# Two blocks of gate and value as plain fp32 products, with the conversions moved behind two root chains

## The chip, the cores and the metric

The kernel runs on one core of a Trainium2 chip. The metric is the device time of one execution in microseconds (us). The engines are TensorE (PE: matmuls; PEld: its weight loads), VectorE (DVE), ScalarE (ACT), GpSimd (POOL) and SyncE (SP, which issues the DMAs).

## The reference

Attention over pooled keys and values, then a gated feed-forward layer behind a root-mean-square norm, then a second feed-forward layer with two factors:

```python
k_p, v_p = mean of 8 neighbouring keys / values         # 576 -> 72 per head
attn = softmax(q @ k_p.T / 8) @ v_p                     # 4 batches, 8 heads, head size 64
x = attn as (2304 tokens, 512)
xn = x / sqrt(mean(x * x) + 1e-6) * rms_g
g = xn @ w_gate;  y = (silu(g) * (xn @ w_val)) @ w_out  # 512 -> 1536 -> 512
out = ((y @ w_a) * (y @ w_b)) @ w_out2                  # 512 -> 1536 -> 512
```

The weights arrive as 64-bit floats. The chip reads each as two 32-bit words and puts an fp32 number together from them.

## The kernel before

The first layer runs over five tiles of 512, 256, 512, 512 and 512 tokens, and in each over 12 blocks f of 128 hidden columns. The attention works in units of 256 tokens; the first tile is made of units 0 and 1, and its left half (`ha`) can be multiplied as soon as unit 0 is scaled.

**Weights.** Block f has three parts (gate, value, out). A part is loaded by SP into one of four staging tiles `st`, and `load_part` can use a tile again only when the conversion four parts earlier has ended. The conversion (`c` in the order list) is two ACT instructions (lines 590 and 591), two on DVE (597 and 600) and one on POOL (607). For the products as three terms, a part is then split (`split_w`, lines 621 and 622) into a high half on ACT and a low half on POOL, or on DVE where the order list writes `!`. The splits have two buffers for gate and two for value.

**Product.** `half` (line 804) multiplies a split weight with split tokens: low by high, high by high, high by low, three matmuls in the reduced type for each 128 rows. Where `f < DIRECT` it multiplies the plain weight with the plain tokens, one fp32 matmul. DIRECT is 0. The first tile's out projection (`out_direct`, line 675) is fp32 already, of the same 128x256 shape in the first four jobs. The jobs 0 to 3 of the first tile are block 0 left, block 1 left, block 0 right, block 1 right; job 4 is block 2 over all 512 tokens, and so on. In the order list g, a, v, h, o stand for the gate product, its silu, the value product, their multiplication on DVE (line 818, into tile `ht`) and the out projection of a job.

**The root chain.** `narrow_rsqrt` (steps V0.6 and V1.6) finds one over the root of the mean square of 256 tokens: three small DVE instructions (478, 481, 485), nine more in three Newton steps (491 to 493), two that make a diagonal (464). V0.7 and V1.7 let PE spread the diagonal (line 472) and then scale the tokens on DVE (line 529). The squares of unit 1 in odd chunks lie in the same buffer `nr` as the diagonal of unit 0. `x0` and `x1` split the scaled tokens of the two units (lines 636 and 637).

**Order.** FIRST lists the steps of the first tile. A step without a sign is free, and its last instruction on each engine becomes the mark; a step with `-` or `=` has its ACT, DVE and POOL instructions put behind the mark of their engine. A planner then orders each engine's queue within these edges, and the engines run their queues in order. `p0` to `p6` pool the second batch's keys and values, the even ones on DVE (line 189), those with `!` on POOL.

Of the kernel before, what the change touches and what calls it, by code (L numbers as in the profile page):

```python
# [20 lines left out]
SLICE = 768  # L21
HALF = SLICE // 2
FINE = 2
DIRECT = 0

# [4 lines left out]
FIRST = """  # L32
=k0 -A0.0@att =k1 l -k2! k3 -l t0@att =A0.1@acc1 A0.2@att w0 =A0.5@acc0 =A0.6@acc3 =A0.7@acc3
-w1 A0.3 =A0.4 w2 t1 =A0.8 A1.0@att A1.1@acc0 A0.9! =c l =A1.2@v -V0.0@acc0 A1.5@acc2 -A1.3
-V0.1@acc1 c A1.6@acc3 s0.0 -V0.2@acc0,v A1.4! -V0.3@g,acc0 =A1.7@acc1 A1.8 A1.9 V0.4@acc2,att
=V0.5@att -c =V1.0@acc0 =V0.6 =V0.7@v =V1.1@g -x0! -g0a V1.2@att,acc3 =V1.3@acc2,acc1 c =g0b
-V1.4@acc0,att =l V1.5@acc2 =V1.6 =V1.7@acc0 s0.1! =c =x1 -a0 s1.0 =v0a =v0b -c =h0 =o0 -g1a
-g1b -s1.1! =c L0 -a1 A2.0 -g2a v1a =L1 -g2b p0 =p1! v1b =c s2.0! h1 =c =a2 =c g3a =c v2a =v2b
-h2 =c g3b =o1 a3 =p2 =o2 -v3a =v3b -s2.1 -h3 g4a g4b p3! -c a4 -v4a s3.0 =c -p4 -v4b s3.1! =c
=o3 =g5a =p5! =c =h4 c -c s4.0! -g5b -c -a5 s4.1! v5a -s5.0 v5b -h5 -g6a -o4 -g6b a6 -p6 -c  # L40
=v6a p7 -s5.1 =v6b -A2.1 -g7a -c =g7b -h6 =c =M0 -c =A2.2 =c -A2.3 =s6.1! =s6.0! -a7 o5 -c v7a
=c =A2.4 v7b s7.0! -h7 -g8a -g8b =a8 -o6 s7.1! c =v8a A2.5 c =s8.0 =p8 v8b =g9a -V2.0 g9b -h8
-a9 -o7 v9a =g10a -s9.0 v9b -c =s8.1 -h9 =c =V2.1 =o8 -V2.2 g10b =s9.1! -a10 -c V2.3 =v10a
-V2.4 -c v10b s10.0 g11a -g11b -h10 =a11 =V2.5 =c -s10.1 =c =o9 -g12a =c -v11a s11.0 =A3.0
=g12b -v11b h11 =a12 -V2.6 -v12a -g13a c -o10 A3.1 -v12b -o11 =g13b -s11.1 =A3.2 -A3.3 =M1
-h12 a13 -v13a -V2.7 -v13b =o12 -h13 =A3.4 =o13 =A3.5
""".split()
SECOND = """
A4.0 =r0 -r1 r2 -r3 r4 -r5 V3.0 r7 =r6 =r8 -V3.1 =V3.2 N0 =V3.3 A4.1 -N1
# [14 lines left out]
def attention_moe_moe2(  # L64
# [715 lines left out]
    def first_tile():  # L780
# [8 lines left out]
        def half(j, part, c0):  # L789
            f, cols, last = jobs[j]  # L790
            if f < DIRECT:
                terms = ((wf[0, f, part], xf_t[0]),)
# [529 lines left out]
```

## Time and profile before

| what | value |
|---|---|
| median of three runs | 1028.63 us (1025.25 to 1029.28) |
| profiled execution, its own time | 1028.68 us |
| its span, first to last instruction | 1026.9 us |
| PE busy | 984.9 us, 96% |
| DVE busy | 608.1 us, 59% |
| ACT busy | 437.9 us, 43% |
| POOL busy | 369.5 us, 36% |
| POOL line 622 (low halves of weights) | 121 instructions, 1366 ns each |

Busy shares are means over the whole run. The stretch that the change touches is about 35 to 90 us, and there the engines stand differently to each other than over the run, so it is read by stretches.

### The profile page before, as it was taken

Reading aid. Unit: us, or ns where it says so; the run is one execution under the profiler, and the core shown is the slowest. Engines: PE = TensorE matmul, PEld = TensorE weight load, DVE = VectorE, ACT = ScalarE, POOL = GpSimd, SP = SyncE. Lnnn points to the kernel's source line nnn. Section 1 sums busy time; section 2 is a strip of 40 time slices with the busy share of each in tenths; the row PEclk is TensorE's granted clock in tenths of the full one; section 3 lists DMA queues with packets and bytes.
Section 4 is the critical chain, followed back from the end, with each engine's and each line's share of the span. In section 5 each row is a group of like instructions: output and inputs, shape, how many; then the busy total and the mean of one; then the engine's idle time right before and its main releaser. Section 6 shows DMA issues by size and latency. Waiting matters only on the chain. (4 is left out here: it accounts for less than half of the span.)

```text
span 1026.9 us, 13276 instructions
## 1 busy us (share of the span) xinstructions
PE 984.9 (96%) x4820; PEld 845.0 (82%) x4820; DVE 608.1 (59%) x963; ACT 437.9 (43%) x822; POOL 369.5 (36%) x301
## 2 busy tenths in 40 slices
PE   4988999999999989999999999999999999999998
PEld 3776676778888877888788899999999998888886
DVE  6898966564733765363627759766776665322221
ACT  3845661232534545444445445434444434331211
POOL 6476672100153433443348620533344333310000
PEclk9889999999999999999999999999999999999999
DMA  8556543320100002000112133444443444643431
GB/s 227 156 175 194 178 140 105 102 78 1 41 1 21 1 1 62 1 1 1 41 28 75 42 111 113 139 148 135 140 151 125 130 129 178 203 140 118 139 113 72
DMA packets 82801, 101.53 MB, mean 99 GB/s; under 512 B 24112, under 2 KB 63024, under 8 KB 82736
## 3 DMA queue, kind: packets, MB, share of 16 engines
q1 hardware_dynamic: 82736, 100.69, 31.7%
q8 instruction: 38, 0.62, 0.2%
q14 instruction: 27, 0.22, 0.1%
HBM read 73.93 MB, written 26.74 MB: 98 GB/s over the span
## 5 line engine op out<-in xcount | busy, mean ns | idle before, releaser
L622 POOL TENSOR_TENSOR wl<-wf,wh 128x512 fp32r<-128x512 f32 x121 | 164.4, 1366 | 263.0 <-ACT wh L621 255.3
L621 ACT CAST wh<-wf 128x512 fp32r<-128x512 f32 x132 | 80.2, 619 | 76.2 <-PE acc L667 27.4
L1103 DVE TENSOR_TENSOR hl<-hf,hh 128x768 fp32r<-128x768 f32 x36 | 35.5, 992 | 95.1 <-ACT hh L1102 95.1
L1125 PE MATMUL o<-woh,hl 128*128 128x512 f32 x216 | 85.8, 397 | 0.0
L1125 PE MATMUL o<-woh,hh 128*128 128x512 f32 x216 | 85.0, 394 | 0.0
L1125 PE MATMUL o<-wol,hh 128*128 128x512 f32 x216 | 84.7, 392 | 0.0
L607 POOL TENSOR_TENSOR w<-w,st 128x512 int32<-128x512 int32 x24 | 31.9, 1330 | 116.0 <-DVE w L600 114.8
L1102 ACT CAST hh<-hf 128x768 fp32r<-128x768 f32 x36 | 29.8, 834 | 91.4 <-PE o L1125 81.5
L675 PE MATMUL acc<-ht,wf 128*128 128x256 f32 (+1 forms) x208 | 67.0, 465 | 1.2 <-DVE ht L818 0.7
L607 POOL TENSOR_TENSOR wf<-wf,st 128x512 int32<-128x512 int32 x36 | 52.9, 1475 | 39.0 <-DVE wf L600 17.3
L1240 ACT ACTIVATE ht<-g 128x512 f32<-128x512 f32 (+1 forms) x48 | 26.1, 544 | 92.8 <-PE g L654 90.2
L1248 DVE TENSOR_TENSOR ht<-ht,v 128x512 f32<-128x512 f32 (+1 forms) x48 | 29.6, 617 | 56.2 <-PE v L654 54.9
L667 PE MATMUL acc<-hh,wl 128*128 128x512 f32 x144 | 57.7, 400 | 3.5 <-ACT hh L1257 3.5
L654 PE MATMUL v<-xh,wl 128*128 128x512 f32 x144 | 57.9, 402 | 0.0
L667 PE MATMUL acc<-hl,wh 128*128 128x512 f32 x144 | 56.8, 394 | 0.1
L654 PE MATMUL g<-xh,wl 128*128 128x512 f32 x144 | 56.7, 394 | 0.0
L667 PE MATMUL acc<-hh,wh 128*128 128x512 f32 x144 | 56.6, 393 | 0.0
L654 PE MATMUL v<-xl,wh 128*128 128x512 f32 x144 | 56.3, 391 | 0.0
L654 PE MATMUL g<-xh,wh 128*128 128x512 f32 x144 | 56.2, 390 | 0.0
L654 PE MATMUL v<-xh,wh 128*128 128x512 f32 x144 | 56.1, 390 | 0.0
L654 PE MATMUL g<-xl,wh 128*128 128x512 f32 x144 | 56.1, 390 | 0.0
L1032 ACT COPY p<-X 128x384 f32<-128x384 f32 x36 | 17.3, 480 | 90.1 <-PE X L1024 90.1
(212 smaller groups left out, 2731.5 us busy)
## 6 DMA issues: line engine op xcount, KB each, us to landing
hf<-h SPq DMA_DIRECT2D x36, 384.0 KB
st<-in_moe_w_out_dram SPq DMA_DIRECT2D x24, 512.0 KB
h<-u SPq DMA_DIRECT2D x36, 192.0 KB
h<-p SPq DMA_DIRECT2D x36, 192.0 KB
st<-in_moe_w_gate_dram SPq DMA_DIRECT2D x12, 512.0 KB
st<-in_moe_w_val_dram SPq DMA_DIRECT2D x12, 512.0 KB
st<-in_moe_w_a_dram SPq DMA_DIRECT2D x12, 512.0 KB
st<-in_moe_w_b_dram SPq DMA_DIRECT2D x12, 512.0 KB
```

The source lines that it names most:

```text
L607: nc.gpsimd.tensor_tensor(out=bits, in0=bits, in1=low, op=ALU.add)
L621: nc.scalar.copy(wh, wf[ph, f, i])
L622: (nc.vector if boot["alt"] else nc.gpsimd).tensor_sub(wl, wf[ph, f, i], wh.bitcast(F32))
L654: nc.tensor.matmul(bank[:, :n], w[:, c, :], x[:, c, cols], start=(i == 0), stop=(i == len(terms) * KD - 1),)
L667: nc.tensor.matmul(accs[c][:, cols], w[:, c, :], x[:, :n], start=(f == 0 and i == 0 and cols.start == 0), stop=(f == NF - 1 and i == 2),)
L675: nc.tensor.matmul(accs[c][:, cols], wf[0, f, 2][:, c, :], ht[:, :cols.stop - cols.start], start=(f == 0 and cols.start == 0), stop=(f == ...
L1032: nc.scalar.copy(t, src[:, :HALF])
L1102: nc.scalar.copy(hh, hf)
L1103: nc.vector.tensor_sub(hl, hf, hh.bitcast(F32))
L1125: nc.tensor.matmul(accs[i], x[:, sub], y, start=(f == 0 and j == 0), stop=(f == NF - 1 and j == 2),)
L1240: act = nc.scalar.activation(out=ht[:, :m], in_=gb[:, :m], func=AF.Silu)
L1248: nc.vector.tensor_mul(ht[:, :m], ht[:, :m], vb[:, :m])
```

## The change

`DIRECT` goes from 0 to 2: jobs 0 to 3 multiply plain fp32 gate and value weights with the plain scaled tokens, one matmul in place of three. The splits of those four parts (s0.0, s0.1, s1.0, s1.1) leave the order list. `x0` and `x1` move from before jobs 0 and 1 to behind job 1's value product, since block 2 is now the first to use split tokens. The steps V0.6, V0.7, V1.6 and V1.7 lose their `=`: they are no longer held behind the mark, and they become it. So all that follows with a sign, the conversions among it, stands behind them, and `p0` gets a sign (`-p0`) and stands behind them too.

```diff
-DIRECT = 0
+DIRECT = 2
...
--V0.1@acc1 c A1.6@acc3 s0.0 -V0.2@acc0,v A1.4! -V0.3@g,acc0 =A1.7@acc1 A1.8 A1.9 V0.4@acc2,att
-=V0.5@att -c =V1.0@acc0 =V0.6 =V0.7@v =V1.1@g -x0! -g0a V1.2@att,acc3 =V1.3@acc2,acc1 c =g0b
--V1.4@acc0,att =l V1.5@acc2 =V1.6 =V1.7@acc0 s0.1! =c =x1 -a0 s1.0 =v0a =v0b -c =h0 =o0 -g1a
--g1b -s1.1! =c L0 -a1 A2.0 -g2a v1a =L1 -g2b p0 =p1! v1b =c s2.0! h1 =c =a2 =c g3a =c v2a =v2b
--h2 =c g3b =o1 a3 =p2 =o2 -v3a =v3b -s2.1 -h3 g4a g4b p3! -c a4 -v4a s3.0 =c -p4 -v4b s3.1! =c
+-V0.1@acc1 c A1.6@acc3 -V0.2@acc0,v A1.4! -V0.3@g,acc0 =A1.7@acc1 A1.8 A1.9 V0.4@acc2,att
+=V0.5@att -c =V1.0@acc0 V0.6 V0.7@v =V1.1@g -g0a V1.2@att,acc3 =V1.3@acc2,acc1 c =g0b
+-V1.4@acc0,att =l V1.5@acc2 V1.6 V1.7@acc0 =c -a0 =v0a =v0b -c =h0 =o0 -g1a -g1b =c L0 -a1
+A2.0 -g2a v1a =L1 -g2b -p0 =p1! v1b =c s2.0! h1 =c =a2 =c -x0! g3a =c v2a =v2b =x1 -h2 =c g3b
+=o1 a3 =p2 =o2 -v3a =v3b -s2.1 -h3 g4a g4b p3! -c a4 -v4a s3.0 =c -p4 -v4b s3.1! =c =o3 =g5a
```

The rest of the list is the same steps in the same order.

## Rows read from the trace of the kernel before

**Rows 1.** Stretches of time: length, each engine's busy us, granted clock, DMA.

```profile
core 0: us, PE busy (x) PEld busy (x) DVE busy (x) ACT busy (x) POOL busy (x), PEclk, DMA share, GB/s
...
56.30:63.10 6.80, 6.28 (x28) 5.81 (x27) 5.27 (x5) 1.52 (x3) 5.55 (x6) 0.50 0.65 195
63.10:75.20 12.10, 12.10 (x75) 10.54 (x73) 11.32 (x17) 8.91 (x17) 7.16 (x6) 1.00 0.53 170
75.20:87.00 11.80, 7.61 (x33) 6.08 (x34) 11.70 (x12) 6.99 (x13) 10.35 (x9) 1.00 0.70 216
...
90.50:112.40 21.90, 21.89 (x94) 14.77 (x93) 17.32 (x26) 10.92 (x18) 13.13 (x10) 1.00 0.64 194
```

**Rows 2.** Waits of PE from 80 to 200 us: total, times, longest.

```profile
PE v L804 <- DVE ht L818: 2.8, 1, 2.8
```

**Rows 3.** Timeline of PE: start, us, instruction, idle before and its releaser.

```profile
54.96 0.70 PE L472 MATMUL rb<-dg,ones 128*128 128x256 f32 x2 [1.99 <-DVE dg L464]
...
67.40 3.62 PE L675 MATMUL acc<-ht,wf 128*128 128x256 f32 x16
...
71.21 0.28 PE L804 MATMUL v<-xh,wl 128*128 128x256 f32 x1
...
72.17 0.28 PE L804 MATMUL v<-xl,wh 128*128 128x256 f32 x1
...
76.62 0.47 PE L804 MATMUL v<-xh,wl 128*128 128x512 f32 x1 [1.42 <-DVE ht L818]
```

**Rows 4.** Timeline of DVE, 34 to 64 us.

```profile
34.86 0.16 DVE L478 TENSOR_SCALAR ba<-sq 128x4 f32<-128x4 f32 x1
...
39.91 0.48 DVE L464 TENSOR_SCALAR dg<-ident,br 128x128 f32<-128x128 f32 x2
...
43.80 0.16 DVE L478 TENSOR_SCALAR ba<-sq 128x4 f32<-128x4 f32 x1 [1.22 <-PE sq L434]
...
57.38 1.21 DVE L529 TENSOR_TENSOR xf<-xf,rb 128x1024 f32<-128x1024 f32 x1
59.28 3.01 DVE L637 TENSOR_TENSOR xl<-xf,xh 128x512 fp32r<-128x512 f32 x2 [0.69 <-ACT xh L636]
63.84 0.42 DVE L818 TENSOR_TENSOR ht<-ht,v 128x256 f32<-128x256 f32 x1 [1.56 <-PE v L804]
```

**Rows 5.** Timeline of DVE, 86 to 164 us.

```profile
86.14 0.68 DVE L818 TENSOR_TENSOR ht<-ht,v 128x512 f32<-128x512 f32 x1
...
98.85 0.43 DVE L597 TENSOR_SCALAR wf<-wf 128x512 int32<-128x512 int32 x1 [4.42 <-ACT wf L590]
...
159.63 0.15 DVE L478 TENSOR_SCALAR ba<-sq 128x4 f32<-128x4 f32 x1
...
163.20 0.48 DVE L464 TENSOR_SCALAR dg<-ident,br 128x128 f32<-128x128 f32 x2
```

**Rows 6.** Groups by form on DVE, 44 to 94 us: count, busy us, mean ns.

```profile
L600 DVE SCALAR_TENSOR_TENSOR wf<-st,wf 128x512 int32<-128x512 int32 x14 | 15.0, 1069 | 0.2
...
L622 DVE TENSOR_TENSOR wl<-wf,wh 128x512 fp32r<-128x512 f32 x5 | 3.4, 683 | 0.0
L491 DVE TENSOR_TENSOR by<-br 128x4 f32<-128x4 f32 x3 | 2.4, 790 | 0.0
...
L492 DVE TENSOR_TENSOR by<-by,ba 128x4 f32<-128x4 f32 x3 | 1.5, 495 | 0.0
```

**Rows 7.** Timeline of ACT: two waits for PE.

```profile
41.18 0.38 ACT L425 ACTIVATE sq<-xT 128x256 f32<-128x256 f32 x1 [1.11 <-PE rb L472]
...
63.54 0.62 ACT L621 CAST wh<-wf 128x512 fp32r<-128x512 f32 x1 [3.78 <-PE g L804]
```

**Rows 8.** Timeline of SP: the load of block 2's out weights.

```profile
43.51 0.34 SPq L572 DMA_DIRECT2D st<-in_moe_w_out_dram  x1
```

**Rows 9.** Timeline of POOL: a split of block 1, a conversion of block 2.

```profile
43.44 1.28 POOL L622 TENSOR_TENSOR wl<-wf,wh 128x512 fp32r<-128x512 f32 x1
...
66.98 1.37 POOL L607 TENSOR_TENSOR wf<-wf,st 128x512 int32<-128x512 int32 x1 [3.57 <-DVE wf L600]
```

More of the change, by code (lines that the diff above doesn't have):

```diff
@@ L34 @@
 -w1 A0.3 =A0.4 w2 t1 =A0.8 A1.0@att A1.1@acc0 A0.9! =c l =A1.2@v -V0.0@acc0 A1.5@acc2 -A1.3
--V0.1@acc1 c A1.6@acc3 s0.0 -V0.2@acc0,v A1.4! -V0.3@g,acc0 =A1.7@acc1 A1.8 A1.9 V0.4@acc2,att
-=V0.5@att -c =V1.0@acc0 =V0.6 =V0.7@v =V1.1@g -x0! -g0a V1.2@att,acc3 =V1.3@acc2,acc1 c =g0b
--V1.4@acc0,att =l V1.5@acc2 =V1.6 =V1.7@acc0 s0.1! =c =x1 -a0 s1.0 =v0a =v0b -c =h0 =o0 -g1a
--g1b -s1.1! =c L0 -a1 A2.0 -g2a v1a =L1 -g2b p0 =p1! v1b =c s2.0! h1 =c =a2 =c g3a =c v2a =v2b
--h2 =c g3b =o1 a3 =p2 =o2 -v3a =v3b -s2.1 -h3 g4a g4b p3! -c a4 -v4a s3.0 =c -p4 -v4b s3.1! =c
[L40 to L46, printed above, removed]
+-V0.1@acc1 c A1.6@acc3 -V0.2@acc0,v A1.4! -V0.3@g,acc0 =A1.7@acc1 A1.8 A1.9 V0.4@acc2,att
[3 more added lines that the diff above has]
+=o1 a3 =p2 =o2 -v3a =v3b -s2.1 -h3 g4a g4b p3! -c a4 -v4a s3.0 =c -p4 -v4b s3.1! =c =o3 =g5a
+=p5! =c =h4 c -c s4.0! -g5b -c -a5 s4.1! v5a -s5.0 v5b -h5 -g6a -o4 -g6b a6 -p6 -c =v6a p7
+-s5.1 =v6b -A2.1 -g7a -c =g7b -h6 =c =M0 -c =A2.2 =c -A2.3 =s6.1! =s6.0! -a7 o5 -c v7a =c
+=A2.4 v7b s7.0! -h7 -g8a -g8b =a8 -o6 s7.1! c =v8a A2.5 c =s8.0 =p8 v8b =g9a -V2.0 g9b -h8 -a9
+-o7 v9a =g10a -s9.0 v9b -c =s8.1 -h9 =c =V2.1 =o8 -V2.2 g10b =s9.1! -a10 -c V2.3 =v10a -V2.4
+-c v10b s10.0 g11a -g11b -h10 =a11 =V2.5 =c -s10.1 =c =o9 -g12a =c -v11a s11.0 =A3.0 =g12b
+-v11b h11 =a12 -V2.6 -v12a -g13a c -o10 A3.1 -v12b -o11 =g13b -s11.1 =A3.2 -A3.3 =M1 -h12 a13
+-v13a -V2.7 -v13b =o12 -h13 =A3.4 =o13 =A3.5
 """.split()
```

## The prediction

> **What bounds the kernel now.** The page says PE, 96% busy over the span, so anything that shortens PE's work or its pauses for good should shorten the run. That is a mean, though, and I first read the table of stretches. From 90.5 to 112.4 us PE is busy 21.89 of 21.90 us, and DVE 17.32. From 75.2 to 87.0 it is the other way round: DVE 11.70 of 11.80, PE only 7.61; from 63.1 to 75.2 both are nearly full [rows 1]. So up to about 87 us the run is bound by DVE, whose queue holds the weight conversions, and after that by PE. Second, PE's waits name the place where the two meet: the value product of block 3 waits 2.8 us for the hidden product `ht` of block 2 [rows 2], which DVE reaches at 86.14 [rows 5]. From 87 us on there is slack on DVE: at 98.85 it has sat idle 4.42 us for ACT [rows 5]. Nothing behind that is set by a clock time of its own, so what DVE gains by 86.14 us, PE keeps to the end, if PE itself can be early by as much.
>
> Third, the DVE timeline shows what is in its queue. The root chain of unit 1 begins at 43.80 and its scaled tokens are there at 58.59, 14.8 us later; in a later unit the same 14 instructions of the chain, with nothing between, take 159.63 to 163.68, 4.05 us [rows 4, 5]. In between stand conversions, pooling, splits. PE waits 1.99 us for the end of that chain [rows 3], and in 56.3 to 63.1 runs at a granted clock of 0.50, the lower level of 1.2 GHz [rows 1].
>
> **The change, part by part.** The sum is made against the profiled execution, 1028.68 us, which is 0.05 us above the median shown.
>
> *PE's work.* Jobs 0 to 3 hold 4 x 2 x 4 = 32 products of 128x256. Three reduced matmuls cost 3 x 0.12 us (nine starts from 71.21 to 72.17 are eight steps in 0.96 us) = 0.36; one fp32 matmul costs 0.216, as 16 of the out projection take 3.62, of which the last is 0.38, so fifteen steps in 3.24 [rows 3]. Saved: 32 x 0.144 = 4.6 us at the full clock.
>
> The Trainium skill, page "FP8 and Floating Point Precision", section "TensorE Precision Notes", says that true FP32 takes four passes through the array. By that one fp32 product would cost four reduced matmuls, 0.48 us, and the change would add 32 x 0.12 = 3.8 us; the sixteen rows at 0.216 each, under two, speak against it.
>
> *PE's pauses.* The 1.99 us before the spreading [rows 3] goes with the shorter chain. The 1.42 us at 76.62, a wait for DVE's `ht` [rows 3], may go. The slow stretch from 56.3 holds 28 matmuls in 6.28 us busy, 0.224 each, against 75 in 12.10, 0.161, in the next at the full clock [rows 1]: 28 x 0.063 = 1.8 us if the clock doesn't fall. In all PE could be early by 4.6 + 2.0 + 1.4 + 1.8 = 9.8 us.
>
> *DVE up to 86.14 us*, which I hold to decide, since it is the later of the two:
> - Two of the four splits are DVE's (s0.1, s1.1): 2 x 0.68 [rows 6] = 1.4 us less. Sure.
> - Two idle times, 0.69 for the cast of unit 1's tokens and 1.56 for a value product of jobs 0 to 3 [rows 4]. Both come from unit 1's late scaling: split tokens were wanted at once. Now nobody in jobs 0 to 3 wants them, and the products come sooner. 0 to 2.25; I take all, as the 22 us behind have no idle row.
> - The chain's Newton steps of unit 1: lines 491 and 492 took 2.4 + 1.5 us for six instructions [rows 6], which are 0.15 each for the same shape when alone [rows 5]: 3.0 us of stretching by what POOL runs beside them. 0 to 3.0; I take 1.8, nearer the upper end, since a chain with no conversion between hands POOL nothing new meanwhile, but what POOL has already begun goes on.
> - Against that DVE now stands while PE spreads the diagonal, since the conversions that filled the time are behind: 0.70 on PE and the hand-over, 0.8 us, for unit 1 surely, for unit 0 only if no free conversion fills it. 0.8 to 1.6; I take 0.8.
> - `x1`'s two instructions took 3.01 us [rows 4] against 0.68 each for the same shape [rows 6]: 1.6 us of stretching, which may or may not return at the new place. 0 to 1.6; half, 0.8.
> - The two POOL splits that go, 1.28 each [rows 9], free POOL; DVE gains where it was stretched by them, seen in line 600's mean of 1069 ns for an instruction shaped like the 683 ns of line 622 [rows 6]. 0 to 2.6; I take 0.6, a quarter.
>
> Sum: 1.4 + 2.25 + 1.8 - 0.8 + 0.8 + 0.6 = 6.0 us; ends -0.2 (1.4 - 1.6) and 10.0.
>
> *What is only moved.* `p0` (two reductions, and the SP load behind it), the splits of `x0` and `x1`, and four conversions (value of block 1, out of block 1, gate and value of block 2) stand behind unit 1's scaling. They cost DVE the same there. Unit 0's chain takes 34.86 to 40.39 now with a conversion inside; alone 4.05, so its scaled tokens come 1.5 us sooner, and with them unit 1's squares, which wait for the buffer that the spreading frees [rows 4, 7]. The value weights of block 1, converted on DVE just before unit 1's chain today, come about 8 us later: 43.80 - 1.5 + 4.05 + 0.8 + 1.21 = 48.4 on DVE instead of 40.3. Queued behind them are PE's value product of job 1 and, on SP, the load that reuses that staging tile: out weights of block 2, issued at 43.51 today [rows 8]. Cover: that part was finished on POOL only at 68.35 [rows 9], 25 us after its load was issued, and PE has 16 products of job 0 and the gate of job 1, about 5 us, in the meantime.
>
> *ACT and the split buffers.* Block 2's split stood in ACT's queue 3.78 us for PE to let go of block 0's buffer [rows 7], and the conversions behind it stood too (POOL's 3.57 us of idle time, [rows 9]). With the splits of blocks 0 and 1 gone the first buffers are free. That helps the conversions reach DVE in time and is the reason why I count no new idle time there; I don't count it twice.
>
> So PE could be 9.8 us early and DVE 6.0: DVE decides, 1028.68 - 6.0 = **1022.7 us**.
>
> **The rivals.**
> - *PE decides.* If the freed buffers and the queue behind let `ht` of block 2 be reached in time, PE's own 9.8 us come through: 1018.9. For it: DVE's 4.42 us of slack behind 94 us. Against: DVE is full from 63 to 87 us.
> - *Hidden.* DVE's stretching and idle times come back elsewhere (POOL runs as many conversions as before), and only the two splits count, less the spreading wait: 0 to 3 us, about 1027. For it: stretching is seen in every stretch.
> - *Slower: the staging loop.* The four held conversions free their staging tiles about 8 us later, so loads of parts 8 to 11 go out later, and each part's conversion frees the tile for the one four behind it. If the 25 us of cover for the out weights of block 2 shrink to under 8 because the queue in front is shorter, the lateness goes round the loop to block 3's and 4's weights, and PE stands for it: 8.0 less the 1.4 saved, 1035.3. Against: that cover.
> - *fp32 at the price of four.* If an fp32 product with these tokens took as long as four reduced matmuls, 4 x 0.12 = 0.48 us, PE's work would grow by 32 x 0.12 = 3.8 us: 1032.5. The sixteen rows of the same shape [rows 3] nearly exclude it.
>
> **How the numbers follow.** Forecast (1020 to 1025) 0.43, PE decides (1014.5 to 1020) 0.20, hidden (1025 to 1030) 0.27, slower 0.08, fp32 dear 0.02. Half a percent, 5.1 us, is about what a measurement of this kernel can tell from no change: under 1023.5 lie PE's case and about four fifths of the forecast's, 0.55; within, the rest and the hidden case, 0.37; slower 0.08. The range takes in the first three cases, 1014.5 to 1030; the unknown terms reach from +0.2 to -10.0 and PE's stretches of lower clock fall where they will.
>
> **What would show it.** Right: in the after trace unit 1's scaling ends on DVE before 50 us; line 804 holds fp32 matmuls of about 0.22 us start to start in jobs 0 to 3; `ht` of block 2 is reached about 6 us sooner, at some 80 us, and PE is full behind it. Wrong: DVE has new idle times between 48 and 80 us; ACT waits for DMA sooner; the loads of block 3 are issued later than today; or PE's first pause has moved to job 1's value product.

## The result, and the profile after

The changed kernel is **slower**: 1036.51 us median (1034.43 to 1037.67) against 1028.14 us for the kernel before, measured beside it, a ratio of 1.0086 with a 95% interval of 1.0069 to 1.0103. That is 8.4 us, where 6 us of gain were forecast. Its profiled execution took 1036.68 us, with a span of 1034.7 us against 1026.9, so 7.8 us of the loss can be looked for in the two traces.

The first thing to read is what the longer span is made of on PE. The line of busy times on the page of after:

```profile
PE 989.8 (96%) x4788; PEld 847.1 (82%) x4788; DVE 608.3 (59%) x961; ACT 435.3 (42%) x818; POOL 366.9 (35%) x299
```

PE is busy 4.9 us longer than before (984.9 us, x4820), although each of 32 products was to become one matmul in place of three, and it is idle 2.9 us longer (1034.7 - 989.8 = 44.9 against 42.0). The count tells why: it should have fallen by 64 and fell by 32. The groups of PE by form, first of after, then of before (the last three numbers: count, busy us, mean ns):

```profile
L804 PE MATMUL g<-xf,wf 128*128 128x256 f32 x32 | 10.9, 486 | 4.6 <-ACT ht L812 4.6
L804 PE MATMUL v<-xf,wf 128*128 128x256 f32 x32 | 10.6, 491 | 0.0
```

```profile
L804 PE MATMUL g<-xl,wh 128*128 128x256 f32 x16 | 6.1, 380 | 0.2 <-DVE xl L637 0.2
```

Jobs 0 to 3 have 4 x 4 = 16 gate products. As reduced matmuls each leaves one record for each of its three terms (x16 for low by high, and so on); as fp32 each leaves **two** (x32). So one fp32 product is two records.

The timeline of PE in after (start, us, instruction, idle before it and its releaser) gives their length, and the pauses:

```profile
45.17 3.76 PE L804 MATMUL g<-xf,wf 128*128 128x256 f32 x8
48.72 0.85 PE L434 MATMUL sq<-ones,sq 128*128 128x2 f32 x4
...
59.35 1.89 PE L804 MATMUL v<-xf,wf 128*128 128x256 f32 x8
65.28 2.08 PE L804 MATMUL g<-xf,wf 128*128 128x256 f32 x4 [4.04 <-ACT ht L812]
...
77.86 3.78 PE L675 MATMUL acc<-ht,wf 128*128 128x256 f32 x8 [4.68 <-DVE ht L818]
...
84.63 0.40 PE L804 MATMUL g<-xh,wh 128*128 128x512 f32 x1
...
86.91 0.39 PE L804 MATMUL g<-xl,wh 128*128 128x512 f32 x1
```

At 59.35 eight records, which are four products, take 1.89 us; the last is 0.38 long, so seven steps in 1.51, 0.216 each: a product costs 2 x 0.216 = 0.43 us, against 0.36 for three reduced ones. Job 0's gate at 45.17 takes 3.76 us, at the lower clock (granted 0.50 from 45.17 to 48.72; 0.71 as the mean of 44 to 54 us, below), and unit 1's last squares (line 434) run only behind it. The two rows with an idle time answer to [rows 3]: PE's longest pauses have grown, and both lie where DVE or ACT is late. By the silu of job 10, the same instruction in both, the whole loss is there: it starts at 139.69 us before and at 148.32 after. From 35 us up to it PE is busy 93.84 and 98.50 us and idle 10.9 and 14.8.

DVE, which the prediction held to decide up to 87 us. Two stretches of time of after, then the same two of before (columns as in [rows 1]):

```profile
44.00:54.00 10.00, 9.20 (x35) 7.75 (x35) 3.34 (x16) 6.80 (x12) 2.46 (x3) 0.71 0.30 86
34.00:90.00 56.00, 43.34 (x166) 34.61 (x167) 45.29 (x73) 28.91 (x58) 29.79 (x23) 0.82 0.45 143
```

```profile
44.00:54.00 10.00, 7.01 (x34) 5.86 (x34) 9.90 (x21) 7.38 (x13) 4.80 (x5) 0.72 0.54 164
34.00:90.00 56.00, 46.32 (x229) 38.91 (x229) 51.68 (x80) 35.70 (x70) 35.85 (x29) 0.85 0.57 174
```

The third busy number is DVE's. Between 44 and 54 us it falls from 9.90 to 3.34, and over the 56 us DVE stands idle 10.7 us in place of 4.3. POOL, the fifth, does 29.79 us in place of 35.85. DVE's timeline in after shows where it stands, and answers to [rows 4, 5]:

```profile
38.14 0.69 DVE L600 SCALAR_TENSOR_TENSOR wf<-st,wf 128x512 int32<-128x512 int32 x1
...
40.31 1.18 DVE L492 TENSOR_TENSOR by<-by,ba 128x4 f32<-128x4 f32 x1
...
41.73 0.48 DVE L464 TENSOR_SCALAR dg<-ident,br 128x128 f32<-128x128 f32 x2
43.01 1.22 DVE L529 TENSOR_TENSOR xf<-xf,rb 128x1024 f32<-128x1024 f32 x1 [0.79 <-PE rb L472]
49.61 0.16 DVE L478 TENSOR_SCALAR ba<-sq 128x4 f32<-128x4 f32 x1 [5.39 <-PE sq L434]
...
55.12 0.76 DVE L597 TENSOR_SCALAR wf<-wf 128x512 int32<-128x512 int32 x2
...
71.70 5.78 DVE L637 TENSOR_TENSOR xl<-xf,xh 128x512 fp32r<-128x512 f32 x2
77.40 0.41 DVE L818 TENSOR_TENSOR ht<-ht,v 128x256 f32<-128x256 f32 x1
```

No conversion runs on DVE between 38.83 and 55.12, 16.3 us, for the conversions stand behind unit 1's scaling; DVE waits 5.39 us for unit 1's squares with nothing it may do meanwhile. And the hidden product at 77.40, for which PE stands 4.68 us, comes behind two token splits that take 5.78 us. What lay beside them, and what feeds the rest, is in POOL's timeline of after:

```profile
38.97 1.29 POOL L607 TENSOR_TENSOR wf<-wf,st 128x512 int32<-128x512 int32 x1 [1.61 <-ACT ef L374]
40.22 1.25 POOL L622 TENSOR_TENSOR wl<-wf,wh 128x512 fp32r<-128x512 f32 x1
...
56.60 3.04 POOL L607 TENSOR_TENSOR wf<-wf,st 128x512 int32<-128x512 int32 x2 [5.61 <-DVE wf L600]
...
69.52 2.85 POOL L180 TENSOR_TENSOR kv<-kv 72x512 f32<-72x512 f32 x2
72.44 0.79 POOL L183 TENSOR_TENSOR kp<-kv 72x128 f32<-72x128 f32 x1
73.19 1.27 POOL L607 TENSOR_TENSOR wf<-wf,st 128x512 int32<-128x512 int32 x1
74.44 2.49 POOL L622 TENSOR_TENSOR wl<-wf,wh 128x512 fp32r<-128x512 f32 x2
```

From 69.52 to 76.93 POOL works with no gap over 0.1 us, and the two splits on DVE end at 77.48. The split at 40.22 is one that neither the diff nor the prediction speaks of: `split_w(ph, f, 2)` (line 1246), the high and low halves of the out weights for the third tile. It bears no sign, so the planner may draw it forward; the expectations below call these splits fillers. In fp32 alone (below) it stands at 39.45 as well, in the kernel before only at 55.18: it moved when the four splits left. DVE's line 492 at 40.31, 0.16 us elsewhere, takes 1.18 us and ends at 41.49, with the split (41.47). Loads, in SP's timeline of after, and the casts of ACT:

```profile
40.28 0.37 SPq L567 DMA_DIRECT2D st<-in_moe_w_val_dram  x1
...
58.24 0.36 SPq L572 DMA_DIRECT2D st<-in_moe_w_out_dram  x1
59.67 0.39 SPq L567 DMA_DIRECT2D st<-in_moe_w_gate_dram  x1
```

```profile
59.68 0.62 ACT L621 CAST wh<-wf 128x512 fp32r<-128x512 f32 x1 [4.45 <-POOL wf L607]
64.33 0.62 ACT L621 CAST wh<-wf 128x512 fp32r<-128x512 f32 x1 [4.03 <-POOL wf L607]
64.85 0.38 ACT L812 ACTIVATE ht<-g 128x256 f32<-128x256 f32 x1
```

The out weights of block 2 are asked for at 58.24, 14.7 us later than in [rows 8]. The cast at 59.68 is again a third-tile split. The one at 64.33 is block 2's own (`s2.0!`; its low half follows on DVE at 64.98). It waits 4.03 us for a conversion, and behind it in ACT's queue stands the silu at 64.85, which PE waits for at 65.28.

### The profile page after: what moved, and what is told of

It is laid out like the page before. It is cut to its first block, busy times and chain, and to the rows that moved or that the text cites. A ratio compares the mean times of both kernels' runs of the same rounds, so it can differ in the third digit from the quotient of the medians.

```text
span 1034.7 us, 13215 instructions
## 1 busy us (share of the span) xinstructions
PE 989.8 (96%) x4788; PEld 847.1 (82%) x4788; DVE 608.3 (59%) x961; ACT 435.3 (42%) x818; POOL 366.9 (35%) x299
## 5 line engine op out<-in xcount | busy, mean ns | idle before, releaser
L621 ACT CAST wh<-wf 128x512 fp32r<-128x512 f32 x128 | 77.8, 619 | 89.8 <-PE acc L667 27.3
L675 PE MATMUL acc<-ht,wf 128*128 128x256 f32 (+1 forms) x208 | 69.1, 478 | 4.9 <-DVE ht L818 4.9
L1102 ACT CAST hh<-hf 128x768 fp32r<-128x768 f32 x36 | 29.8, 834 | 91.8 <-PE o L1125 82.0
L675 PEld LDWEIGHTS acc<-ht,wf 128*128 128x128 f32 x208 | 40.6, 198 | 24.9 <-issue 15.2
```

Source lines behind the costliest of these rows:

```text
L621: nc.scalar.copy(wh, wf[ph, f, i])
L675: nc.tensor.matmul(accs[c][:, cols], wf[0, f, 2][:, c, :], ht[:, :cols.stop - cols.start], start=(f == 0 and cols.start == 0), stop=(f == ...
L1102: nc.scalar.copy(hh, hf)
```

## The experiments

All ratios are to the kernel before, measured beside each run, with 95% intervals. A sign in the order list (`-`, `=`) puts a step behind the mark of its engine, as described under Order above. The runs are numbered e1 to e16. To hold, here, is to keep all conversions behind unit 1's scaling.

**fp32 alone** (e1). Order of before, the four splits out, DIRECT = 2.

```diff
-DIRECT = 0
+DIRECT = 2
...
--V0.1@acc1 c A1.6@acc3 s0.0 -V0.2@acc0,v
+-V0.1@acc1 c A1.6@acc3 -V0.2@acc0,v
...
-s0.1! =c =x1 -a0 s1.0 =v0a =v0b -c =h0 =o0 -g1a -g1b -s1.1!
+=c =x1 -a0 =v0a =v0b -c =h0 =o0 -g1a -g1b
```

> DIRECT = 2 and the four splits out, everything else in the order of before (chains signed, x0 and x1 early, p0 free). Theory HELD (the conversions that stand behind unit 1's root chain starve the loads): nothing is held, so 3 to 8 us under before, 1020 to 1025 us. Theory FP32 (the fp32 products, 0.43 us each at the lower clock, stand in front of unit 1's squares and delay all behind): at least 4 us over before, 1032 or more. Theory TOKENS (the moved token splits, 5.8 us on DVE at their new place): under before, as they are not moved.

1028.99 us, 1.0006 (0.9990 to 1.0022). PE's busy time is 985.5 us, 0.6 more than before, and the span the same. fp32 in itself shows neither gain nor loss here; the interval reaches up to 0.22%, 2.3 us.

**The hold alone** (e2). Three terms as before, the chains free and what has a sign behind them.

```diff
-=V0.6 =V0.7@v
+V0.6 V0.7@v
...
-=V1.6 =V1.7@acc0 s0.1!
+V1.6 V1.7@acc0 -s0.1!
...
-p0
+-p0
```

> DIRECT stays 0 with all splits; only the order of the chains changes: V0.6, V0.7, V1.6, V1.7 free, p0 and s0.1 signed, so that all conversions stand behind unit 1's chain on DVE. HELD: 6 to 12 us over before, 1034 to 1040, with loads stopping between about 40 and 55 us. FP32 and TOKENS: within 3 us of before, since neither is in it.

1031.33 us, 1.0034 (1.0017 to 1.0051): a loss clear of noise, but about half of the least that was expected (6 us).

**The changed kernel without the hold** (e3; the four steps signed again, the rest as changed).

```diff
-V0.6 V0.7@v
+=V0.6 =V0.7@v
...
-V1.6 V1.7@acc0
+=V1.6 =V1.7@acc0
```

> The changed kernel with the four chain steps signed again, so that conversions may stand in between; fp32 products and late token splits stay. HELD: 1020 to 1028. FP32: 1033 or more. TOKENS: 1033 or more.

1032.96 us, 1.0051 (1.0031 to 1.0071): the hold is worth 1.0086 / 1.0051, 0.35% here too, but more than half of the loss is left.

**The changed kernel with early token splits** (e4).

```diff
-=V1.1@g -g0a
+=V1.1@g -x0! -g0a
...
-=c -a0
+=c =x1 -a0
...
-=c -x0! g3a =c v2a =v2b =x1 -h2
+=c g3a =c v2a =v2b -h2
```

> The changed kernel with the token splits x0 and x1 back at their old places; the hold and the fp32 products stay. TOKENS: back to 1026 to 1030, the 5.8 us on DVE at 72 to 77 gone. HELD and FP32: 1033 to 1038.

1034.91 us, 1.0068 (1.0044 to 1.0093). The interval overlaps that of the changed kernel; by itself this run shows only that the late token splits are not the whole loss, as TOKENS had it. None of the three theories stands alone after these four runs.

**Unit 1's squares ahead of job 0's gate** (e5).

```diff
-=V1.1@g -g0a V1.2@att,acc3 =V1.3@acc2,acc1 c =g0b -V1.4@acc0,att =l V1.5@acc2
+=V1.1@g V1.2@att,acc3 =V1.3@acc2,acc1 c -V1.4@acc0,att =l V1.5@acc2 -g0a =g0b
```

> The changed kernel with the gate product of job 0 listed behind unit 1's last squares, so that PE sums the squares first (one fp32 matmul stays in front instead of four). Theory SQUARES (fp32 products at the lower clock, 0.43 us each, stand in front of the last squares; DVE, whose conversions are held, idles 5.4 us): 3 to 4 us under the changed kernel, about 1033. If the hold costs the same wherever PE sums: within 2 us of 1036.

1032.70 us, 1.0039 (1.0020 to 1.0057). DVE's idle time ahead of unit 1's chain falls from 5.39 to 2.83 us, and the time by 3.8. So a part of the loss lies in that wait, and a part of the wait is the fp32 gate of job 0 at the lower clock, which in the changed kernel stood before the squares.

**The third-tile splits put behind the marks**, in fp32 alone (e6), in the changed kernel (e7) and in the kernel before (e8):

```diff
             if own and idx > 1:
-                split_w(ph, f, 2)
+                run(lambda: split_w(ph, f, 2), "-")
```

> fp32_only (e1) with the out-weight splits of the third tile put behind their marks, so that they can't be drawn forward into ACT's and POOL's queues at 38 to 60 us. Theory FILL (those two splits took the place of the removed ones, stretch unit 0's chain and stand in front of the silu): 4 to 8 us under before, 1020 to 1025. Otherwise within 2 us of e1, 1027 to 1031.

> The changed kernel with the third tile's out-weight splits put behind their marks. FILL: 3 to 5 us under the changed kernel, 1031 to 1034, the 4.0 us pause of PE at 61 us gone. Otherwise within 2 us of 1036.

> The kernel before with the third tile's out-weight splits put behind their marks: what that edit does by itself. FILL: within 3 us of before, as there the two splits ran at 51 to 60 us, beside a DVE chain that nobody on PE was near. If it is under before by as much as e6, the edit helps any order and says nothing of the change.

1024.45 us, 0.9954 (0.9939 to 0.9969); 1030.67 us, 1.0027 (1.0011 to 1.0043); 1024.80 us, 0.9965 (0.9948 to 0.9983). These splits had a price in the kernel before already, 0.35%. It is 0.52% with fp32 and 0.59% in the changed kernel; that the change made it dearer is what the middle values say, but their difference, 0.24%, is about as large as the intervals. Two of the three versions (e6, e8) beat both kernels, and between these two fp32 is worth nothing that shows. The theory behind e7 had the time right and one sign wrong: PE's pause for the silu was to go, and is still 2.38 us, behind the same cast of block 2, which waits 7.45 us for its conversion. What e7's trace has instead is a unit 1 that is scaled by 51.37 us and not 55.20, with job 0's gate at the full clock (1.97 us for its eight records, not 3.76).

**Late token splits alone** (e9): fp32 alone, with `x0` and `x1` at the changed kernel's places; no hold, `p0` free.

```diff
--x0! -g0a
+-g0a
...
-=x1 -a0
+-a0
...
-=c g3a =c v2a =v2b -h2
+=c -x0! g3a =c v2a =v2b =x1 -h2
```

> fp32 alone (1028.99 us), with the splits of the tokens x0 and x1 put at the changed kernel's places behind job 1's products; the chains stay held behind marks, conversions lie between them, p0 is free. Without the hold, fp32 together with late token splits and the signed p0 took 1032.96, 0.4% more than fp32 alone. Theory: that 4 us is the token splits', which meet back-to-back work of POOL at their new place and hold up the hidden product and block 2's products; then this run takes 1032 to 1034, and the DVE timeline shows the x splits of line 637 at 3 us or more for two. Rival: it is p0's (pooling moved among the conversions) or needs the two together; then this run takes 1029 to 1030.

1033.57 us, 1.0050 (1.0034 to 1.0066), so 0.44% over fp32 alone, with nothing else moved. It also equals the changed kernel without the hold, which has `p0` signed besides: `p0` is worth nothing that shows. DVE's timeline, first with the early places (`x1`'s two), then with the late ones (all four):

```profile
64.37 1.28 DVE L637 TENSOR_TENSOR xl<-xf,xh 128x512 fp32r<-128x512 f32 x2
```

```profile
65.97 3.47 DVE L637 TENSOR_TENSOR xl<-xf,xh 128x512 fp32r<-128x512 f32 x2
69.69 1.76 DVE L637 TENSOR_TENSOR xl<-xf,xh 128x512 fp32r<-128x512 f32 x1
73.07 0.68 DVE L637 TENSOR_TENSOR xl<-xf,xh 128x512 fp32r<-128x512 f32 x1
73.67 0.41 DVE L818 TENSOR_TENSOR ht<-ht,v 128x256 f32<-128x256 f32 x1
```

Four splits of 0.68 us take 5.91 us at the late places, and a hidden product stands right behind them.

**The hold with its company taken away** (e10): the changed kernel with the squares ahead, the third-tile splits behind and the token splits early, all three edits from above.

> The changed kernel with three of its side effects taken out: job 0's gate behind unit 1's last squares, third-tile out-weight splits behind the marks, token splits at the old places. What stays of the change is fp32, the two chains together with the conversions behind, and the signed p0. To be set beside fp32 with the splits behind the marks (1024.45). Theory: standing conversions cost about 0.35% by themselves, since the staging loop starts late, so 1027 to 1029, with no load issued by SP for about 15 us. Rival: the hold was dear only through what it met (the squares, the fillers, the token splits), and with these out the shorter chains pay: 1020 to 1024.5.

1031.19 us, 1.0023 (1.0013 to 1.0033). Against fp32 with the third-tile splits behind (e6, 0.9954) that is 0.69%, 7 us. The nearer counterpart is e12 below, which has job 0's gate behind the squares too and differs in the hold and `p0` alone: against its 0.9967 the hold costs 0.56%, 5.7 us. Here I had expected 1027 to 1029: the hold has a price without the three things that it met.

**The hold without fp32 and without fillers** (e16): the hold alone with the third-tile splits behind.

> The kernel before with the third-tile splits behind the marks (1024.80) and the two chains together with the conversions behind them, as in the hold alone (1031.33 with the fillers in front): three terms, no fp32, token splits early. Theory: holding costs by the standing loads whatever the fillers do, 1028 to 1030. Rival: it was dear because the filler splits stretched the chain and stood in ACT's queue, 1024 to 1026.

1031.24 us, 1.0033 (1.0019 to 1.0048), against 0.9965 without the hold: 0.68%, now with three terms. SP's loads, first of the kernel before with the fillers behind, then of this run, which issues no weight load for 16 us:

```profile
42.68 0.34 SPq L572 DMA_DIRECT2D st<-in_moe_w_out_dram  x1
```

```profile
38.60 0.37 SPq L567 DMA_DIRECT2D st<-in_moe_w_val_dram  x1
54.59 0.36 SPq L572 DMA_DIRECT2D st<-in_moe_w_out_dram  x1
```

What DVE does in these two, first the kernel before with the fillers behind (e8), then with the hold (e16): the stretch from 34 to 90 us, and the two DVE lines of the conversions from 44 to 94 us.

```profile
34.00:90.00 56.00, 46.16 (x238) 37.94 (x236) 52.16 (x84) 33.78 (x65) 37.31 (x29) 0.94 0.62 188
L600 DVE SCALAR_TENSOR_TENSOR wf<-st,wf 128x512 int32<-128x512 int32 x14 | 14.1, 1010 | 0.2
L597 DVE TENSOR_SCALAR wf<-wf 128x512 int32<-128x512 int32 x15 | 11.9, 795 | 3.1 <-ACT wf L590 3.1
```

```profile
34.00:90.00 56.00, 44.77 (x218) 37.77 (x219) 51.84 (x79) 30.88 (x60) 32.99 (x26) 0.85 0.52 162
L600 DVE SCALAR_TENSOR_TENSOR wf<-st,wf 128x512 int32<-128x512 int32 x14 | 17.6, 1256 | 0.2
L597 DVE TENSOR_SCALAR wf<-wf 128x512 int32<-128x512 int32 x15 | 12.7, 849 | 0.0
```

DVE is busy as long in both, 52.16 and 51.84 us, but the same 29 conversion instructions take 30.3 us in place of 26.0. So here the hold's price is not more idle time of DVE: the conversions come later and take longer where they now stand. The other pairs read alike. From 34 to 90 us DVE is busy 51.84 us in e2 and 51.68 before, 52.03 in e10 and 53.24 in e12; and the conversions' two lines, from 44 to 94 us, take 29.8 us for 29 instructions in e2 and 26.8 for 28 before, 30.1 for 28 in e10 and 25.5 for 30 in e12. Why they take longer there, these runs do not test.

**One conversion back between the chains**: in the changed kernel (e11), and with the third-tile splits behind as well (e14).

```diff
-V0.6 V0.7@v =V1.1@g
+V0.6 V0.7@v =c =V1.1@g
...
-V1.6 V1.7@acc0 =c -a0
+V1.6 V1.7@acc0 -a0
```

> The changed kernel with the one conversion that stood right behind unit 1's scaling listed between the two chains instead (behind unit 0's scaling), where DVE stood idle 5.39 us. Theory (the staging loop starts late): one part more is converted and one load more goes out about 10 us sooner, and the time falls by 2 to 4 us, to 1032.5 to 1034.5. Rival (the hold costs by the place of the chain, not by the standing conversions): the chain of unit 1 starts on its squares as before and nothing behind it is sooner, 1036 to 1037; or later, if the conversion stretches the chain, up to 1038.

> The changed kernel with one conversion listed between the two chains (1028.25 us) and also the third-tile out-weight splits put behind the marks (which alone took the changed kernel from 1036.5 to 1030.67). Theory: the two share a part, since with the conversion between the filler split fell behind unit 0's chain anyway; the rest of the fillers' cost is in ACT's queue, where a cast waits 4.0 us for a conversion ahead of job 1's silu, and that is still there: 1025.5 to 1027. Rival (the conversion freed all there was): 1028 to 1029. Rival (the two add up): 1022 to 1023.

1028.25 us, 0.9998 (0.9985 to 1.0010), and 1024.58 us, 0.9971 (0.9957 to 0.9984). One conversion listed at another place takes back 8.3 us, far more than the 2 to 4 I had expected, and all that the change had lost. e14 falls between its theory and the rival in which the two add up. In e11 two things move at once: the third-tile split also falls behind unit 0's chain. In e14 against e7 both have that split behind, and the conversion alone is still worth 0.9971 / 1.0027, 0.56% or 5.8 us. Unit 1's chain starts at nearly the same time in the two, and these rows show what has changed, of e14 first SP, then DVE, then PE:

```profile
44.22 0.34 SPq L572 DMA_DIRECT2D st<-in_moe_w_out_dram  x1
```

```profile
45.58 0.16 DVE L478 TENSOR_SCALAR ba<-sq 128x4 f32<-128x4 f32 x1 [2.76 <-PE sq L434]
```

```profile
70.12 3.66 PE L675 MATMUL acc<-ht,wf 128*128 128x256 f32 x8 [2.30 <-DVE ht L818]
```

and the same pause of PE in e7:

```profile
72.63 3.56 PE L675 MATMUL acc<-ht,wf 128*128 128x256 f32 x8 [7.38 <-DVE ht L818]
```

The load goes out at 44.22, although DVE reaches unit 1's chain only at 45.58 (44.89 in e7), because one more conversion has run between the two chains; in e7 it went out at 54.42. PE's pause for the hidden product behind the token splits is 2.30 us in place of 7.38, and its idle time from 34 to 140 us 10.9 in place of 17.5. DVE is not less idle for it: from 34 to 90 us it is busy 50.95 us in e14 and 50.52 in e7.

**Job 0's gate behind the squares, without the hold** (e12).

```diff
-=V1.1@g -x0! -g0a V1.2@att,acc3 =V1.3@acc2,acc1 c =g0b -V1.4@acc0,att =l V1.5@acc2
+=V1.1@g -x0! V1.2@att,acc3 =V1.3@acc2,acc1 c -V1.4@acc0,att =l V1.5@acc2 -g0a =g0b
```

> fp32 with the third-tile out-weight splits behind the marks (1024.45), and job 0's gate product put behind unit 1's last squares. Theory: in fp32 with conversions between the chains DVE is idle only 1.62 us before unit 1's chain, and the squares stand behind job 0's gate only in part, so little is left to gain: 1023 to 1025. Rival: unit 1's scaling is what holds DVE's queue in this stretch, and sooner squares bring the whole 1.6 us and the stretched Newton steps: 1020 to 1022.5. The other way: job 0's hidden product comes later and with it PE's first pause, 1025 to 1027.

1024.96 us, 0.9967 (0.9955 to 0.9980): nothing gained over e6, as expected. The sooner squares gained time in e5, where DVE may do nothing else while it waits, and not here.

**The price of fp32 by itself** (e13): the kernel before, with blocks 6 and 7 in fp32, where PE is full.

```diff
-            if f < DIRECT:
+            if f in (6, 7):
...
-=c -A2.3 =s6.1! =s6.0! -a7 o5 -c v7a =c =A2.4 v7b s7.0! -h7
+=c -A2.3 -a7 o5 -c v7a =c =A2.4 v7b -h7
...
-=a8 -o6 s7.1! c
+=a8 -o6 c
```

> The kernel before with blocks 6 and 7 (not 0 and 1) as plain fp32 products and without their four splits, where PE has no idle time over 0.15 us from 113.56 us to 172 us: the price of fp32 by itself. 16 products of 128x512 stand for 48 reduced ones of 0.229 us each start to start. Theory from the trace of the changed kernel, where 16 fp32 products left 32 records: each fp32 product is two records, so 2 x about 0.43 = 0.86 us against 0.69, PE's work grows by about 2.8 us, and the time by 2 to 3 us, less at most 1.2 us of a pause that ended with a split of one of these blocks: 1029 to 1031. Rival, the prediction's reading (one record for a product): 0.43 against 0.69, PE gains 4.1 us, 1023 to 1025.

1034.78 us, 1.0065 (1.0049 to 1.0081). Slower, as by two records, and by more than their price. PE's timeline:

```profile
111.86 3.59 PE L804 MATMUL g<-xf,wf 128*128 128x512 f32 x8
115.29 3.60 PE L675 MATMUL acc<-ht,wf 128*128 128x512 f32 x8
...
133.56 2.91 PE L804 MATMUL v<-xf,wf 128*128 128x512 f32 x4 [4.15 <-DVE ht L818]
```

Four products take 115.29 - 111.86 = 3.43 us, 0.86 each. Three reduced ones of this shape are 0.68: in after's timeline ten steps lie between 84.63 and 86.91, 0.228 each. That is 16 x 0.17 = 2.8 us more work. The rest is a new pause of 4.15 us for a hidden product, so as a time this run shows the direction only; the price stands in its rows.

**Four blocks in fp32** (e15), the third-tile splits behind.

```diff
-DIRECT = 2
+DIRECT = 4
...
-v1b =c s2.0! h1
+v1b =c h1
...
-=v3b -s2.1 -h3 g4a g4b p3! -c a4 -v4a s3.0 =c -p4 -v4b s3.1! =c
+=v3b -h3 g4a g4b p3! -c a4 -v4a =c -p4 -v4b =c
```

> fp32 with the third-tile splits behind the marks (1024.45), with four blocks in fp32 in place of two: blocks 2 and 3 too, their four splits out (two on DVE, two on POOL), the token splits at their old early places. PE's work grows by 2 blocks x 2 x 4 products x 0.17 = 2.8 us, DVE's falls by 1.4 and POOL's by some 2.6 to 3. Theory: up to the end of block 3 DVE and POOL decide and PE has pauses of some 7 us to hide it in, so this gains 1 to 3 us: 1021.5 to 1023.5. Rival: PE is not idle enough behind 77 us, the fp32 work comes out in full: 1026 to 1027.5.

1026.22 us, 0.9973 (0.9959 to 0.9987), against 0.9954 with two blocks. The gain of 1 to 3 us did not come; between no change and 2.8 us more the run doesn't tell.

## Why the prediction was wrong

**PE's work: the sign was wrong.** The prediction took the sixteen fp32 rows at 67.40 [rows 3] for sixteen products. They are eight: the out projection has four matmuls in a job, and they belong to two jobs. So a product costs 2 x 0.216 = 0.43, not 0.216, and the saving of 4.6 us is 32 x 0.07 = 2.3 us more work. The count stood in the trace of before: line 675 has 128 records of 128x256, and the program issues 64 (4 in each of jobs 0 to 3, 4 in each of the second tile's 12 blocks). In fp32 alone PE's busy time rose by 0.6 us and not by 2.3; its mean granted clock was 0.988 in place of 0.986, and by the working under **PE's pauses and clock** that is an estimated 2 us less of work. So that run shows fp32 even as a time, not that the 2.3 us are free.

That also turns the rival that was given 2 chances in 100. The prediction cited the Trainium skill, page "FP8 and Floating Point Precision", section "TensorE Precision Notes", on four passes for true FP32, and held that the rows speak against it. By that rule a product is an estimated 0.48 us; measured is 0.43, or 3.6 reduced matmuls, and 0.86 to 0.228, or 3.8, at 512 columns. The trace comes close to the rule, and the prediction's reading was off by two.

**DVE up to 86 us.** That DVE decides there held in part, in the bad sense: it reaches the first 512-wide `ht` at 90.92 in place of 86.14, 4.8 us of the 7.8 that the span lost. The rest comes behind it; one piece is a pause of PE of 2.16 us at 114.26, for queries of the attention, that the kernel before doesn't have. Term by term, by after's groups of DVE by form from 44 to 94 us, which answer to [rows 6]:

```profile
L600 DVE SCALAR_TENSOR_TENSOR wf<-st,wf 128x512 int32<-128x512 int32 x12 | 11.5, 966 | 0.1
L637 DVE TENSOR_TENSOR xl<-xf,xh 128x512 fp32r<-128x512 f32 x4 | 8.2, 2079 | 0.0
...
L491 DVE TENSOR_TENSOR by<-br 128x4 f32<-128x4 f32 x3 | 0.6, 208 | 0.1
```

- *Newton steps of unit 1, 1.8 us gain:* came, and more. Line 491's three take 0.6 us in place of 2.4, line 492's 0.5 in place of 1.5.
- *POOL's splits, 0.6:* came. Line 600's mean falls from 1069 to 966 ns, 1.2 us for twelve.
- *Two idle times, 2.25:* both are gone, but new ones of 5.39, 0.79 and 0.79 us in the chains stand for them. This term failed worst. Nobody had asked what DVE does while unit 1's squares are computed: before, conversions filled that time, and the change forbids them to. The prediction counted the standing for the two spreadings alone, at 0.8 us.
- *x1's stretch, 0.8 gain:* the other way. Line 637 takes 8.2 us for four, against 4.3 before; four at 0.68 are 2.7. By e9 the late places cost 0.44% by themselves.
- *Unit 0's chain alone, 1.5 us sooner:* it runs from 35.11 to 42.21, 7.1 us, longer than the 5.5 of before. One conversion and the second half of another still lie inside, POOL's work beside them, and last the third-tile split.

So the gains that were named came in part, and the stretched token splits took them back: over the whole run DVE is busy 608.3 us, as before (608.1). What is new in the changed kernel is the standing: in 34 to 90 us DVE gets through 73 instructions in place of 80, idle 6.4 us more.

**What is only moved, at nothing.** This is the second step that failed. The 25 us of cover were real for the load: it went out 14.7 us late, not 8, and still ACT waits for no weight load between 40 and 95 us in after. What had no cover was the conversions' own time on DVE and POOL: 16 us without one on DVE, four parts to be made up by an engine that is the bound, and "they cost DVE the same there" was wrong. That the hold has a price is shown by e2, e10 and e16 (0.34, 0.56 and 0.68%, e10 against e12) and, the other way, by e14 (one conversion back, 0.56%). How it is paid is shown in part: not through more idle time of DVE, except in the changed kernel itself, but through the same conversions taking 3 to 5 us more of DVE's time where they now stand. The rival "staging loop" had the size (1035.3) and the standing conversions, but by luck: its path, PE waiting for late loads, isn't what the rows show in after. In e2 and e16 ACT does wait for weight loads, 6.2 and 6.5 us from 40 to 95 us, but it does so without the hold too (7.5 before, 6.7 in e8; none in after); the longest single wait is longer with it (3.0 and 3.3 us against 1.8 and 1.9), so as a part of the price in those runs the loop isn't excluded.

**Freed split buffers.** They helped nobody whom the prediction named: the casts of block 2 wait for their conversions instead. The third-tile splits came forward, on POOL beside unit 0's chain (40.22) and at 60.37, for 2.24 us, between two conversions. e7 put them back, for 5.8 us.

**PE's pauses and clock.** The waits for the two spreadings stayed, 2.9 us in all in both kernels; the 1.42 and the 2.8 for `ht` went, and 4.04, 4.68 and 2.16 came. The term of 1.8 us for the clock was read from two stretches of unlike matmuls: rows of one shape, 128x256 reduced, start 0.213 us apart at the lower level (57.07 to 57.71 in the kernel before) and 0.12 at the full one, which makes it 28 x 0.093 = 2.6. It did not come either way. The mean granted clock fell from 0.986 to 0.984, instead of rising: with the lower level at half speed, an estimated 2 x (0.016 x 1034.7 - 0.014 x 1026.9) = 4.4 us more at that level, 2.2 us of work; the third digit of the clocks leaves about 1 us either way open. With fp32's 2.3 us and the 2.9 us of pauses that makes 7.4 of the span's 7.8.

**What would show it.** Of the signs that the prediction gave, unit 1's scaling ends at 55.2 us, not before 50; the first 512-wide `ht` of DVE comes at 90.92, not 80; DVE has new idle times in 48 to 80; the loads of block 3 begin at 59.67, later. Line 804 does show 0.22 us from start to start, and that sign was no test, since it counted records.

**The loss in parts.** Edit by edit from the kernel before: fp32 0.06% (e1), the late token splits 0.44% more (e9, and e3 with `p0` signed), the hold 0.35% more (after), 0.86% in all. In the other order the hold costs 0.62% on top of fp32 (e4 against e1) and the late splits 0.18% on top of that, which is within the intervals. So fp32 carries none of the loss that shows, and the two moves share it, dividing it differently by their order.

What stays **open**: by the middle values the hold costs 0.34% beside the fillers' early splits and 0.56 to 0.68% without them, and single edits of the changed kernel (e5, e7, e11) give back 3.8, 5.8 and 8.3 us of a loss of 8.4. The parts overlap, and the runs don't divide them further. Whether the third-tile splits are dearer under the change than before is not settled either.

## What to carry to other kernels

Before a record's length is multiplied by a count of operations, count the records against the instructions that the program issues; one fp32 product was two records here. And work that is "only moved" on the engine that sets the pace has a price of its own, whatever cover its inputs have: price it at the length that it has beside its new neighbours, not at its old one. Four token splits went from 4.3 to 8.2 us by their new place, and the conversions of the held runs from 26.0 to 30.3. One conversion put back into the gap took back the whole loss (e11), and splits that an automatic order may draw forward were worth 0.35% in the kernel before, by one line (e8, 1024.80 us; e6 and e14, 1024.45 and 1024.58, are not told apart from it).

## What was not expected of the hardware

In the changed kernel one DVE split, 0.68 us elsewhere, took 4.64 us (the longer of the two in the row at 71.70). It ran beside POOL instructions of which no single one is longer than 1.5 us, with no gap over 0.1 us between them, and ended 0.55 us after the last. Beside single POOL instructions, DVE's 0.16 us steps of unit 0's chain took 1.14 to 1.18 us and ended within 0.02 us of POOL's. So in these traces a DVE instruction is lengthened not by one POOL instruction only but by a run of them. That POOL is what holds DVE is inferred from these times; no run takes POOL's work away by itself.

Four executions of the changed kernel had mean granted clocks of 0.983 to 0.984 (1036.35 to 1037.67 us) and of 0.988 (1034.43 us): some 2 to 3 us between executions of one kernel go with PE's clock.
